# Transposing q and k by DMA as 16-bit halves, from the fifth pair of heads on

## The chip, the cores and the metric

The kernel runs on one core of a Trainium2 chip. The metric is the device time of one execution in microseconds (us), lower is better. Before the change the median of three runs is 1266.16 us (1265.27 to 1266.54).

## The reference

Attention that keeps only the 32 largest scores of each row, followed by a small network on the result. There are 8 batches, 8 heads, 576 positions and 64 values per head.

```python
scores = 1/sqrt(64) * q @ k.T                  # (8, 8, 576, 576)
kth    = 32nd largest score of each row
attn   = softmax(scores where scores >= kth)
x      = (attn @ v), heads side by side        # (4608, 512)
h      = max(x @ w1, x @ w2, x @ w3)           # (4608, 768)
out    = h @ w_out                             # (4608, 512)
```

## The kernel before

**Tiling.** Heads are worked on in pairs: with 64 values per head, two heads fill the 128 partitions. Each pair has four units of 128 query rows; the 64 rows left over of two pairs make a fifth unit. That is 144 units in all. For a unit, TensorE computes the scores of both heads into PSUM (`qk`, L531), ScalarE copies them to SBUF (`evac`, L539), VectorE and GpSimd find the 32nd largest value (the lines up to L614), VectorE masks (L637), ScalarE takes the exponential (L646), TensorE transposes the result with an identity matrix (`turn`, L692), ScalarE copies the transposes out (L704), and TensorE multiplies with v (`values`, L723). Three small steps after it (L733 on VectorE, L747 on ScalarE, L751 on GpSimd) put the attention result into x as two 16-bit parts. When all heads of a batch have done a span of rows, the network runs on the span: L780 is its first layer, L840 the second, L845 and L851 write the result.

**What the change touches: preparing q and k.** The scores need q and k with the 64 values of a head along the partitions. Today `load_qk` brings both from memory as they lie (L445; L449 for the last 64 rows), and `prep` returns three steps. Step one transposes the last rows on TensorE (L474) and copies them out (L477). The two others, for k and then for q, are four transposes each on TensorE (L483), a scaled copy from PSUM into the one buffer `raws` (L487), a rounding copy into `kT` or `qT` (L488), and a subtraction on GpSimd that leaves the rounding error (L492). The score product uses both parts. `kT` and `qT` have two buffers; `raws`, `qt`, `kt` and `last` have one. A pair is prepared once, but those of the first batch twice, so there are 36 preparations, which `prepare(pi)` numbers in order.

**What sets the order.** The program is not written in order of time. Every step is a `Piece` with an engine, an estimated cost, the steps that it needs, the ring buffers that it takes and a rank (the unit that it belongs to, plus a number of `OFFSETS` by kind of step). `in_order` plays the pieces on a model of the five engines, and the order in which the model starts them is the order of each engine's instructions. Every engine, and SP, which issues all transfers, then works in that order, whatever the real times are. The model takes a result of another engine to be seen after the step's cost, that engine's `LATE` (2000 ns for SP) and `GAP`. The pieces of the network are a list of their own (`fill`): on TensorE they are looked at last, so they take the time that attention leaves.

**End.** The units of the last batch are ordered so that its first 256 rows are complete first, then the next 256, then the last 64. The network on these three spans ends the program.

Of the kernel before, what the change touches and what calls it, by code (L numbers as in the profile page):

```python
# [8 lines left out]
F32 = mybir.dt.float32  # L9
F32R = mybir.dt.float32r  # L10
F16 = mybir.dt.float16
BF16 = mybir.dt.bfloat16
I32 = mybir.dt.int32
AF = mybir.ActivationFunctionType
ALU = mybir.AluOpType
AX = mybir.AxisListType
# [8 lines left out]
NSSB = 5  # L25
NWB = 6
PMB = 2
GAP = 104.0
NEAR = 162.0
SWITCH = 95.0  # L30
WINDOW = 150
LEAD = 42.7
LOCK_A = -150.0
LOCK_B = -100.0
OFFSETS = {'E0': -5.5, 'E1': 2.05, 'E2': 2.82, 'N': -0.93, 'T0': 0.58, 'T1': 5.15, 'T2': 2.73, 'Y': -1.06, 'Z': -0.03, 'd': -3.25,
# [8 lines left out]
RANK_M = -20.0  # L44
LATE = {'PE': 160.0, 'DVE': 85.0, 'ACT': 100.0, 'POOL': 40.0, 'SP': 2000.0}

# [21 lines left out]
def in_order(pieces, fill):  # L68

    queues, fills = {e: [] for e in LATE}, {e: [] for e in LATE}
    for x in sorted(pieces, key=lambda x: x.rank):
        queues[x.engine].append(x)
    for x in fill:
        fills[x.engine].append(x)
    free = {e: 0.0 for e in LATE}
    mode, shut = [None], [0.0]

    def ready(x):  # L80
        t = free[x.engine]
        for y in x.needs:
            if y.start is None:
                return None
            t = max(t, y.seen(x.engine))
        ahead = {}
        for ring, releases in x.takes:
            k = len(ring.users) - ring.size + ahead.get(ring, 0)
            ahead[ring] = ahead.get(ring, 0) + 1
            for y in ring.users[k] if k >= 0 else ():  # L90
                if y.start is None:
                    return None
                t = max(t, y.seen(x.engine))
        if x.engine == "PE" and x.mode != mode[0]:
            t += SWITCH

        if x.alone:
            t = max(t, free["POOL"] + LOCK_A)
        elif x.engine == "POOL":
            t = max(t, shut[0] + LOCK_B)  # L100
        return t

    left = len(pieces) + len(fill)
    while left:
        best = None
        low = min((q[0].rank for q in queues.values() if q), default=0.0)
        for e in LATE:
            some = [x for x in queues[e][:WINDOW] if x.rank <= low + LEAD]
            some = some + fills[e][:1] if e == "PE" else fills[e][:1] + some
            could = [(t, x) for x in some if (t := ready(x)) is not None]  # L110
            if could:
                first = min(t for t, _ in could) + PATIENCE[e]
                t, x = next(c for c in could if c[0] <= first)
                if best is None or t < best[0]:
                    best = t, x
        assert best, [(e, len(q), len(fills[e])) for e, q in queues.items()]
        t, x = best
        (fills if fills[x.engine][:1] == [x] else queues)[x.engine].remove(x)
        x.start = t
        free[x.engine] = t + x.cost  # L120
        if x.engine == "PE":
            mode[0] = x.mode
        if x.alone:
            shut[0] = t + x.cost
        for ring, releases in x.takes:
            ring.users.append(releases)
        x.run()
        left -= 1


PATIENCE = {'PE': 97, 'DVE': 158, 'ACT': 0, 'POOL': 0, 'SP': 0}


@with_exitstack
def kernel(ctx, tc, q, k, v, moe_w1, moe_w2, moe_w3, moe_w_out, out):
# [8 lines left out]
    KC = DM // P  # L144
    FC = DF // P
    HALF = S // 2
    HALF_SCALE = (SHRINK / float(D) ** 0.5) ** 0.5
    MAIN = NU * P
    WIDE = S - 2 * P
    HW = WIDE + 64  # L150
# [311 lines left out]
    def prep(b, hp):  # L462
# [11 lines left out]
            nc.tensor.transpose(pt[:, 0:P], both[2].rearrange("p h d -> p (h d)"), ident)  # L474

        def rest_out():
            nc.scalar.activation(raws[:, S:].rearrange("p (w n) -> p w n", n=64)[:, ::C], box["rest"][:, 0:P].rearrange("p (w n) -> p w n", w=2), AF.Copy,  # L477
                                 scale=HALF_SCALE)

        def products(w):  # L480
            pt = box[w] = ps_t.tile([P, 512], F32, name="tr")
            for c in range(NU):
                nc.tensor.transpose(pt[:, c * P:(c + 1) * P], both[w][:, c].rearrange("p h d -> p (h d)"), ident)  # L483

        def split(w):
            raw, t = (raw_of_q, raw_of_k)[w], (qT[:, 0, 0:S + 64], kT[:, 0])[w]
            nc.scalar.activation(raw[:, 0:MAIN], box[w], AF.Copy, scale=HALF_SCALE)  # L487
            nc.scalar.copy(t, raw)  # L488

        def rest_of(w):  # L490
            raw, t, low = (raw_of_q, raw_of_k)[w], (qT[:, 0, 0:S + 64], kT[:, 0])[w], (qT[:, 1, 0:S + 64], kT[:, 1])[w]
            nc.gpsimd.tensor_tensor(low, raw, t.bitcast(F32), ALU.subtract)  # L492
        return [(rest, rest_out, None)] + [(lambda w=w: products(w), lambda w=w: split(w), lambda w=w: rest_of(w)) for w in (1, 0)]

    which = [1]
    spots = const.tile([P, NW], F32, name="spots")
# [37 lines left out]
    def evac(n):  # L534
        d = st[n]
        s = d["s"]
        t = wk.tile([P, 2, S], F32, name="ssb", bufs=NSSB)
        d["ssb"] = [t[:, 0], t[:, 1]]
        nc.scalar.copy(t.rearrange("p h (i n) -> p h i n", i=2), s[:, :, :, :HALF])  # L539

    def sweep(n, i):

# [363 lines left out]
    def attention(n):  # L906
# [17 lines left out]
            opened[b] = []  # L924
            takes.append(("books", opened[b]))
        p("q", "PE", 786 if full else 1572, lambda: qk(n), needs=[x for k in preps_of[n] for x in prepared[k]], takes=takes, mode="rows")
        p("e", "ACT", 1060, lambda: evac(n), needs=[d["q"]], takes=[("ssb", held(n, "ssb"))])
        rel.append(d["e"])
        for i in range(2):
            p(("s", i), "DVE", 1184 - 296 * i, lambda i=i: sweep(n, i), needs=[d["e"]] + ([d["s", 0]] if i else []),  # L930
# [86 lines left out]
    def prepare(pi):  # L1017
        b, hp = preps[pi]
        rank = starts[pi]
        load = piece("SP", 4000, lambda: load_qk(b, hp), list(load_last), rank, tag="ql" if pi else "ql0")  # L1020
        box = {}
        load_last.clear()
# [2 lines left out]
        for k in range(3):  # L1025
# [3 lines left out]
                box["turns"][k][0]()  # L1029
            rel = []  # L1030
            x = piece("PE", 140 if k == 0 else 436, products, [load, *done[-1:]], rank, [("tr", rel)], tag="qp")
            y = piece("ACT", 220 if k == 0 else 1206, lambda k=k: box["turns"][k][1](), [x, *last, *done[-1:]], rank, tag="qp")
            rel.append(y)
            load_last.append(x)
            if pi >= 2:
# [5 lines left out]
                load_bits.append(z)  # L1041
        prepared[pi] = done

    load_bits = []

    def finish(b):
# [120 lines left out]
```

## Time and profile before

| | |
|---|---|
| median of 3 runs | 1266.16 us |
| the profiled execution | 1265.52 us |
| its span, first to last instruction | 1263.8 us |
| TensorE (PE) busy | 1190.5 us, 94% |
| VectorE (DVE) busy | 1139.0 us, 90% |
| ScalarE (ACT) busy | 1057.1 us, 84% |
| GpSimd (POOL) busy | 927.2 us, 73% |
| mean granted TensorE clock | 0.988 of 2.4 GHz |

The busy times are sums over the span, which has three parts that differ: about 100 us of start, in which the weights are brought in and converted, a long even stretch, and an end in which TensorE works alone. PEld is TensorE's loading of weights, which runs beside its products. Durations of TensorE's instructions overlap, so what one of them costs is the distance from its start to the start of the next, not its length.

### The profile page before, as it was taken

What the parts mean: (1) busy time and instruction counts of PE and PEld (TensorE: products, weight loads), DVE (VectorE), ACT (ScalarE), POOL (GpSimd) and SP (SyncE); (2) the same over time, 40 slices, a digit from 0 to 9 for tenths busy, and PEclk for the clock granted to TensorE, in tenths of its full rate; (3) what the DMA queues carried; (4) which work ended last, traced back from release to release, by engine and by line L of the source; (5) the groups of instructions that cost most, each with busy time, mean ns of one, the idle gap of its engine ahead of it and who ended that gap; (6) DMA issues with size and microseconds to landing.
All of it is one profiled execution on the core that took longest, in us unless ns stands there. A gap on an engine that the chain in (4) does not pass through costs nothing.

```text
span 1263.8 us, 32126 instructions
## 1 busy us (share of the span) xinstructions
PE 1190.5 (94%) x10431; PEld 882.2 (70%) x10431; DVE 1139.0 (90%) x5558; ACT 1057.1 (84%) x2382; POOL 927.2 (73%) x1443
## 2 busy tenths in 40 slices
PE   4677789999999999999999999999999999999997
PEld 2455567878686766767687777867776767767775
DVE  7899999999999999999999999999999999999221
ACT  2799899999998988899899999898998889888321
POOL 1667778788888786878878788877787888868111
PEclk9999899999999999999999999999999999999999
DMA  8440111111111110011111111100110111000000
GB/s 274 140 139 20 38 38 49 39 38 38 38 30 46 30 38 27 21 50 26 46 30 46 30 39 46 30 28 20 53 42 28 30 29 37 2 18 2 18 18 29
DMA packets 112401, 54.86 MB, mean 43 GB/s; under 512 B 96608, under 2 KB 104800, under 8 KB 112224
## 3 DMA queue, kind: packets, MB, share of 16 engines
q1 hardware_dynamic: 112224, 52.72, 15.2%
q8 instruction: 84, 1.38, 0.4%
q14 instruction: 93, 0.76, 0.2%
HBM read 43.25 MB, written 9.44 MB: 42 GB/s over the span
## 4 chain that ended last, share of the span: by engine, by line
PE 71%; DVE 17%; ACT 8%; issue 2%; POOL 1%; DMA 1%; SPq 0%; ACTq 0%; DVEq 0%; POOLq 0%
PE m L780 28%; PE tr L723 11%; PE s L531 10%; PE m L840 10%; PE tr L692 8%; DVE L L548 4%; DVE ssb L637 4%; DVE Q L596 2%; PE tr L483 2%; ACT pm L646 2%; ACT w L587 2%; PE tr L687 1%; ACT pT L704 1%; DVE h L789 1%; ACT ssb L539 1%
## 5 line engine op out<-in xcount | busy, mean ns | idle before, releaser
L592 POOL TENSOR_TENSOR w<-ssb,w 128x576 f32<-128x576 f32 x288 | 425.9, 1485 | 51.4 <-ACT w L587 47.7
L780 PE MATMUL m<-xh,wall 128*128 128x256 f16 (+4 forms) x2592 | 441.7, 273 | 2.2 <-DVE h L789 1.3
L780 PEld LDWEIGHTS <-wall 128*128 128x128 f16 x3888 | 354.5, 98 | 76.4 <-issue 11.7
L780 PE MATMUL m<-xl,wall 128*128 128x256 f16 (+4 forms) x1296 | 345.1, 273 | 0.0
L548 DVE MAX8 L<-ssb 128x8 f32<-128x82 f32 (+1 forms) x2016 | 317.2, 227 | 3.1 <-ACT ssb L539 3.1
L637 DVE SCALAR_TENSOR_TENSOR ssb<-ssb,kth 128x576 f32<-128x576 f32 x288 | 262.3, 923 | 0.2
L646 ACT ACTIVATE pm<-ssb,nb 128x576 f32<-128x576 f32 x288 | 224.5, 781 | 29.8 <-DVE ssb L637 29.3
L704 ACT COPY pT<-tr 128x512 f32<-128x512 f32 (+1 forms) x432 | 215.0, 515 | 31.6 <-PE tr L692 17.9
L587 ACT ACTIVATE w<-ssb,Q 128x576 f32<-128x576 f32 x288 | 223.0, 777 | 14.2 <-DVE Q L580 12.2
L596 DVE MAX8 Q<-w 128x8 f32<-128x576 f32 x288 | 214.1, 748 | 5.0 <-POOL w L592 4.7
L692 PE MATMUL tr<-ident,pm 128*128 128x128 f32 x1152 | 179.3, 282 | 11.4 <-ACT pm L646 6.6
L531 PE MATMUL s<-kT,qT 64*128 64x288 f32 x1920 | 173.1, 316 | 14.4 <-ACT ssb L539 8.5
L723 PE MATMUL tr<-pT,vt 128*64 128x256 f32 (+2 forms) x2000 | 179.3, 328 | 2.7 <-ACT s L192 1.9
L531 PEld LDWEIGHTS s<-kT,qT 64*128 64x128 f32 x1920 | 137.7, 192 | 58.8 <-ACT ssb L539 19.5
L539 ACT COPY ssb<-s 128x1152 f32<-128x1152 f32 x144 | 161.5, 1121 | 14.5 <-PE s L531 13.7
L789 DVE SCALAR_TENSOR_TENSOR h<-m,rises,h 128x256 f32<-128x256 f32 (+4 forms) x216 | 102.8, 476 | 74.5 <-PE m L780 68.5
L692 PEld LDWEIGHTS tr<-ident,pm 128*128 128x128 f32 x1152 | 131.3, 142 | 51.4 <-issue 14.6
L723 PEld LDWEIGHTS tr<-pT,vt 128*64 128x64 f32 x2000 | 112.0, 139 | 60.8 <-issue 13.3
L795 POOL TENSOR_TENSOR hl<-h,hh 128x256 f16<-128x256 f32 (+4 forms) x108 | 83.8, 776 | 83.8 <-ACT hh L792 82.8
L840 PE MATMUL m<-wall,hh 128*128 128x512 f16 x432 | 128.6, 379 | 0.0
L661 POOL TENSOR_SCALAR rsw<-rs 128x128 f32<-128x128 f32 x144 | 62.1, 431 | 27.9 <-DVE rs L656 10.8
L840 PE MATMUL m<-wall,hl 128*128 128x512 f16 x216 | 81.9, 379 | 0.0
(124 smaller groups left out, 1648.9 us busy)
## 6 DMA issues: line engine op xcount, KB each, us to landing
qt<-in_q_dram SPq DMA_DIRECT2D x72, 128.0 KB, 2.8
kt<-in_k_dram SPq DMA_DIRECT2D x72, 128.0 KB, 3.0
out_dram<-ob SPq DMA_DIRECT2D x32, 256.0 KB, 2.3
wall<-in_moe_w_dram SPq DMA_DIRECT2D x8, 768.0 KB, 6.2
vt<-in_v_dram SPq DMA_DIRECT2D x32, 128.0 KB, 2.1
vt<-in_v_dram SPq DMA_DIRECT2D x32, 64.0 KB, 2.2
vt<-in_v_dram SPq DMA_DIRECT2D x96, 16.0 KB, 2.0
vt<-in_v_dram SPq DMA_DIRECT2D x32, 48.0 KB, 2.1
```

The costliest lines, as they stand in the source:

```text
L531: nc.tensor.matmul(s[:, h, i, :HALF], qT[sl, qa, c0:c0 + P], kT[sl, ka, i * HALF:(i + 1) * HALF], start=(n_ == 0 and a == 0), stop=(n_ == ...
L548: nc.vector.max(d["L"][:, t, g, :], d["ssb"][t][:, g * S // G:(g + 1) * S // G])
L587: nc.scalar.activation(d["w"][t], d["ssb"][t], AF.Sign, bias=d["Q"][:, t, 0:1], scale=-1.0, accum_out=d["cnt"][:, t:t + 1])
L592: nc.gpsimd.tensor_tensor(d["w"][t], d["ssb"][t], d["w"][t], ALU.mult)
L596: nc.vector.max(d["Q"][:, t, 1:NW], d["w"][t])
L637: nc.vector.scalar_tensor_tensor(ss, ss, d["kth"][:, t:t + 1], ss, ALU.is_lt, ALU.subtract, accum_out=d["lost"][:, t:t + 1])
L646: nc.scalar.activation(d["pm"][:, t], d["ssb"][t], AF.Exp, bias=d["nb"][:, t:t + 1], scale=-1.0 / SHRINK, accum_out=d["sums"][:, t:t + 1])
L692: nc.tensor.transpose(pt[:, j * P:(j + 1) * P], pm[:, i, 64 * i + j * P:64 * i + (j + 1) * P], ident)
L704: nc.scalar.copy(pT[:, 512 * i:512 * i + m] if i < 2 else pT[:, 8 * P:10 * P], pt[:, :m])
L723: nc.tensor.matmul(xp[64 * h:64 * h + 64, to], vt[:, 4 * h + i if i < 4 else 8 + h, :], keys, start=(i == 0), stop=(i == 4))
L780: nc.tensor.matmul(box["ps", i][:, :c1 - c0], a, bb[:, kc, c0:c1], start=(kc == 0 and k == 0), stop=(kc == KC - 1 and k == 2))
L840: nc.tensor.matmul(box["po"][:n], a[:, f, cs], bb, start=(f == 0 and k == 0), stop=(f == FC - 1 and k == 2))
```

## The change

From preparation 4 on (`BY_DMA = 4`, so 32 of 36), TensorE no longer transposes q and k. Instead, for k and then for q:

- `load`: SP issues two transposing transfers, one per head. The 576x64 32-bit numbers are read as 576x128 16-bit numbers and arrive as 128x576, with the low halves of the numbers in the even partitions and the high halves in the odd ones.
- `gather`: SP issues four transfers from SBUF to SBUF, which collect the low halves and the high halves of both heads in one tile `halves` of 128 partitions x 2 x 576.
- `split`: ScalarE joins the halves in `raws` by two copies of 16-bit numbers, of 1024 and of 128 per partition.
- `high`, `low`: the rounding copy on ScalarE and the subtraction on GpSimd, as before.

The two transposed tiles and `halves` have one buffer each. The factor that was put on q and on k (its square root on each) goes on the scores, in the copy from PSUM. The order's constants and all `OFFSETS` are set anew, and TensorE in a mode (the score products, the products with v) prefers to stay in it for up to `STICK` ns of the model.

```diff
-GAP = 104.0
-NEAR = 162.0
-SWITCH = 95.0
+GAP = 106.0
+NEAR = 167.0
+SWITCH = 100.0
+STICK = 191.0
-LEAD = 42.7
+LEAD = 62.6
...
-                first = min(t for t, _ in could) + PATIENCE[e]
-                t, x = next(c for c in could if c[0] <= first)
+                first = min(t for t, _ in could)
+                stays = [c for c in could if c[1].mode and c[0] <= first + STICK] if e == "PE" and mode[0] else []
+                t, x = stays[0] if stays else next(c for c in could if c[0] <= first + PATIENCE[e])
...
-PATIENCE = {'PE': 97, 'DVE': 158, 'ACT': 0, 'POOL': 0, 'SP': 0}
+PATIENCE = {'PE': 103, 'DVE': 161, 'ACT': 16, 'POOL': 21, 'SP': 0}
...
-            nc.scalar.activation(raw[:, 0:MAIN], box[w], AF.Copy, scale=HALF_SCALE)
+            nc.scalar.copy(raw[:, 0:MAIN], box[w])
...
+        def load(w):
+            tiles = box["tiles"] = [io.tile([P, S], U16, name=nm, bufs=1) for nm in ("qt", "kt")]
+            for h in range(2):
+                nc.sync.dma_start(tiles[h], (q, k)[w][b, 2 * hp + h].bitcast(U16), transpose=True)
+
+        def gather(w):
+            both = box["both"] = io.tile([P, 2, S], U16, name="halves", bufs=1)
+            for h in range(2):
+                for t in range(2):
+                    nc.sync.dma_start(both[64 * h:64 * h + 64, t, :], box["tiles"][h][t::2, :])
+
+        def split(w):
...
+            words = raw.bitcast(U16)
+            nc.scalar.copy(words[:, 0:2 * MAIN].rearrange("p (c n t) -> p c n t", c=NU, t=2),
+                           both[:, :, 0:MAIN].rearrange("p t (n c) -> p c n t", c=NU))
+            end = raw.shape[1]
+            nc.scalar.copy(words[:, 2 * (end - 64):2 * end].rearrange("p (n t) -> p n t", t=2), both[:, :, MAIN:S].rearrange("p t n -> p n t"))
...
-        nc.scalar.copy(t.rearrange("p h (i n) -> p h i n", i=2), s[:, :, :, :HALF])
+        nc.scalar.activation(t.rearrange("p h (i n) -> p h i n", i=2), s[:, :, :, :HALF], AF.Copy, scale=SCALE)
...
-        p("e", "ACT", 1060, lambda: evac(n), needs=[d["q"]], takes=[("ssb", held(n, "ssb"))])
+        p("e", "ACT", 1170, lambda: evac(n), needs=[d["q"]], takes=[("ssb", held(n, "ssb"))])
...
+        if pi >= BY_DMA:
+            steps = turned_prep(b, hp)
+            done, last, before = [], list(load_bits), list(load_last)
+            load_bits.clear()
+            for w in (1, 0):
+                load, gather, split, high, low = ((lambda f=f, w=w: f(w)) for f in steps)
+                x = piece("SP", 4300, load, before, rank, tag="ql")
+                y = piece("SP", 3000, gather, [x, *free_halves], rank, tag="qm")
+                before = [y]
+                z = piece("ACT", 1150, split, [y, *last, *done[-1:]], rank, tag="qs")
+                users[pi - 2].append(z)
+                free_halves[:] = [z]
+                h = piece("ACT", 610, high, [z], rank, tag="qp")
+                lo = piece("POOL", 1420, low, [h], rank, tag="qp")
+                done += [h, lo]
+                load_bits.append(lo)
+            load_last[:] = before
+            prepared[pi] = done
+            return
```

## Rows read from the trace of the kernel before

**Rows 1.** By stretch: busy PE, PEld, DVE, ACT, POOL (instructions); clock, DMA share, GB/s.
```profile
100.00:1150.00 1050.00, 1019.61 (x9046) 760.28 (x9046) 1014.92 (x5078) 950.65 (x2148) 849.47 (x1316) 0.99 0.13 34
...
1181.00:1259.00 78.00, 75.18 (x739) 58.33 (x737) 16.33 (x43) 17.10 (x42) 10.33 (x19) 1.00 0.06 20
```

**Rows 2.** The chain that ended last, from 1181 us: start, us, what.
```profile
1183.79 20.96 PE m L780 x192
1204.75 7.77 PE m L840 x36
1212.52 23.58 PE m L780 x216
1236.10 7.79 PE m L840 x36
```

**Rows 3.** By stretch, L780 alone: busy PE, PEld (instructions); clock, DMA share, GB/s.
```profile
1153.00:1181.00 28.00, 10.03 (x67) 6.24 (x66) 1.00 0.03 11
```

**Rows 4.** The same with L840 alone.
```profile
1153.00:1181.00 28.00, 8.59 (x36) 3.51 (x36) 1.00 0.03 11
```

**Rows 5.** Timeline: the last step of the last batch's first 256 rows.
```profile
1152.81 1.17 POOL L751 TENSOR_TENSOR xl<-xs,xh 128x256 f16<-128x256 f32 x1 [0.71 <-ACT xh L747]
```

**Rows 6.** Timeline of PE: the transposes of q and k, each with its successor.
```profile
597.09 0.60 PE L483 MATMUL tr<-ident,kt 128*128 128x128 f32 x4
...
597.53 0.43 PE L780 MATMUL m<-xh,wall 128*128 128x320 f16 x2
...
626.71 0.27 PE L474 MATMUL tr<-ident,last 128*128 128x128 f32 x1
...
626.82 0.59 PE L840 MATMUL m<-wall,hh 128*128 128x512 f16 x2
```

**Rows 7.** The transposes of q: ns min/median/max, first and last start, shape.
```profile
L483 PE MATMUL tr<-ident,qt x144: 271/273/421, 18.5 to 1088.6; 128*128 128x128 f32 x144
```

**Rows 8.** Groups of ACT, shapes apart: busy us, mean ns, idle before and releaser.
```profile
L704 ACT COPY pT<-tr 128x512 f32<-128x512 f32 x288 | 166.2, 584 | 25.9 <-PE tr L692 17.9 <-DVE xs L733 4.6 <-DVE kth L614 1.4
L539 ACT COPY ssb<-s 128x1152 f32<-128x1152 f32 x144 | 161.5, 1121 | 14.5 <-PE s L531 13.7
L487 ACT ACTIVATE raws<-tr 128x512 f32<-128x512 f32 x72 | 43.1, 599 | 11.5 <-PE tr L483 11.0
L845 ACT ACTIVATE ob<-m,so 128x512 f32<-128x512 f32 x32 | 22.1, 692 | 14.2 <-PE m L840 14.1
L477 ACT ACTIVATE raws<-tr 128x128 f32<-128x128 f32 x36 | 10.4, 288 | 16.7 <-PE tr L474 16.7
```

**Rows 9.** Who waited for whom on DVE and ACT, 100 to 1150 us: us, times, longest.
```profile
DVE h L789 <- PE m L780: 15.1, 37, 1.3
DVE xs L733 <- PE tr L723: 5.1, 9, 1.6
ACT pm L646 <- DVE ssb L637: 28.4, 34, 2.7
ACT w L587 <- DVE Q L580: 11.5, 14, 3.1
ACT raws L487 <- PE tr L483: 6.9, 12, 1.1
```

**Rows 10.** DMA issues: KB each, median us from issue to landing.
```profile
qt<-in_q_dram SPq DMA_DIRECT2D x72, 128.0 KB, 2.8
vt<-in_v_dram SPq DMA_DIRECT2D x32, 64.0 KB, 2.2
```

**Rows 11.** Timeline of SP: one load of q and k.
```profile
612.75 1.25 SPq L445 DMA_DIRECT2D qt<-in_q_dram  x2
```

**Rows 12.** DMA queue: packets, MB, share of 16 engines.
```profile
q1 hardware_dynamic: 112224, 52.72, 15.2%
```

**Rows 13.** One line of each batch's review: first and last start, for the batch period.
```profile
L669 DVE TENSOR_TENSOR junk<-Q,kth x8: 476/492/1599, 207.6 to 1171.0; 128x324 f32<-128x324 f32 x8
```

**Rows 14.** Who waited for whom on SP's queue: us in total, times, longest.
```profile
SPq L851 <- ACT ob L845: 206.4, 23, 37.2
```

More of the change, by code (lines that the diff above doesn't have):

```diff
@@ L13 @@
 I32 = mybir.dt.int32
+U16 = mybir.dt.uint16
 AF = mybir.ActivationFunctionType
@@ L27 @@
 PMB = 2
-GAP = 104.0
-NEAR = 162.0
-SWITCH = 95.0
+GAP = 106.0
+NEAR = 167.0
+SWITCH = 100.0
+STICK = 191.0
 WINDOW = 150
-LEAD = 42.7
+LEAD = 62.6
 LOCK_A = -150.0
 LOCK_B = -100.0
-OFFSETS = {'E0': -5.5, 'E1': 2.05, 'E2': 2.82, 'N': -0.93, 'T0': 0.58, 'T1': 5.15, 'T2': 2.73, 'Y': -1.06, 'Z': -0.03, 'd': -3.25,
[8 rows of a table removed]
+OFFSETS = {'E0': -6.34, 'E1': -0.03, 'E2': 1.48, 'N': -1.36, 'T0': -2.57, 'T1': 6.25, 'T2': 2.95, 'Y': 1.38, 'Z': -0.59, 'd':
[9 rows of a table added]
 RANK_M = -20.0
@@ L146 @@
     HALF = S // 2
-    HALF_SCALE = (SHRINK / float(D) ** 0.5) ** 0.5
+    SCALE = SHRINK / float(D) ** 0.5
     MAIN = NU * P
@@ L476, in rest_out @@
         def rest_out():
-            nc.scalar.activation(raws[:, S:].rearrange("p (w n) -> p w n", n=64)[:, ::C], box["rest"][:, 0:P].rearrange("p (w n) -> p w n", w=2), AF.Copy,
-                                 scale=HALF_SCALE)
+            nc.scalar.copy(raws[:, S:].rearrange("p (w n) -> p w n", n=64)[:, ::C], box["rest"][:, 0:P].rearrange("p (w n) -> p w n", w=2))
         def products(w):
@@ L493, in prep, with turned_prep, high, low @@
         return [(rest, rest_out, None)] + [(lambda w=w: products(w), lambda w=w: split(w), lambda w=w: rest_of(w)) for w in (1, 0)]
+    def turned_prep(b, hp):
+        box = {}
+        def load(w):
[8 more added lines that the diff above has]
+        def split(w):
+            if w:
+                which[0] ^= 1
+                T_of[b, hp] = qTs[which[0]], wk.tile([P, 2, S], F32R, name="kT")
+            both = box["both"]
+            raw = (raw_of_q, raw_of_k)[w]
+            words = raw.bitcast(U16)
[3 more added lines that the diff above has]
+            nc.scalar.copy(words[:, 2 * (end - 64):2 * end].rearrange("p (n t) -> p n t", t=2), both[:, :, MAIN:S].rearrange("p t n -> p n t"))
+        def high(w):
+            qT, kT = T_of[b, hp]
+            nc.scalar.copy((qT[:, 0, 0:S + 64], kT[:, 0])[w], (raw_of_q, raw_of_k)[w])
+        def low(w):
+            qT, kT = T_of[b, hp]
+            to, t = (qT[:, 1, 0:S + 64], kT[:, 1])[w], (qT[:, 0, 0:S + 64], kT[:, 0])[w]
+            nc.gpsimd.tensor_tensor(to, (raw_of_q, raw_of_k)[w], t.bitcast(F32), ALU.subtract)
+        return load, gather, split, high, low
     which = [1]
@@ L1031, in prepare @@
             x = piece("PE", 140 if k == 0 else 436, products, [load, *done[-1:]], rank, [("tr", rel)], tag="qp")
-            y = piece("ACT", 220 if k == 0 else 1206, lambda k=k: box["turns"][k][1](), [x, *last, *done[-1:]], rank, tag="qp")
+            y = piece("ACT", 160 if k == 0 else 1080, lambda k=k: box["turns"][k][1](), [x, *last, *done[-1:]], rank, tag="qp")
             rel.append(y)
@@ L1042, in prepare @@
         prepared[pi] = done
+    BY_DMA = 4
+    free_halves = []
     load_bits = []
```

17 rows, old and new, of the table OFFSETS are left out of this document.

## Prediction

> **What bounds the kernel now.** I read the busy time by stretch first, because the page's shares are averages over a start, an even stretch and an end. From 100 to 1150 us PE is busy 1019.6 of 1050 us, DVE 1014.9, ACT 950.7 and POOL 849.5 [rows 1]: two engines at 97%, ACT at 91%. From 1181 us on DVE and ACT are nearly idle and PE has 75.2 of 78 us [rows 1]. The chain of waits says what that end is: first layer and second layer of the network on 256 rows (20.96 and 7.77 us), on the next 256 rows (23.58 and 7.79), and a short one on the last 64 [rows 2]. So when attention ends, at 1181 us, the whole network of the last batch is still to do.
>
> It is still to do because the network takes only what attention leaves of PE, and PE has been behind: between 1153 and 1181 us it spends 10.0 us in L780 and 8.6 us in L840 [rows 3, 4], and those belong to the batch before. The last batch's first 256 rows are complete only with the subtraction that starts at 1152.81 us [rows 5]. The end is thus set by two things, the moment at which attention ends (DVE, with ACT close behind) and the work that PE has left by then.
>
> **What PE loses.** In the timeline four transposes of k start at 597.09 us and the next instruction at 597.53, so four cost 0.44 us though each is listed with more; the one of the last rows costs 0.11 us (626.71 to 626.82) [rows 6]. A preparation has two fours and one single: 0.99 us. 32 of 36 preparations lose them: 31.7 us of PE, all before 1089 us, where the last of them starts [rows 7]. The stickiness in a mode may save some more; no row prices it, and by what follows PE could not use it.
>
> **What of it is worth time.** With attention's own times kept, the freed PE time goes to the network, which then reaches the last batch earlier. But the last batch's first rows cannot be used before 1153 us. To be free for them then, PE must have done the 18.6 us of older network work (10.0 + 8.6) that now lies between 1153 and 1181. Of the 31.7 us freed, 18.6 do this; the other 13.1 become idle time before 1153. In its place 18.6 us of the last batch's first layer move in front of 1181 us, and the end comes 18.6 us earlier. I take 1 us off for the beginning of that layer, which now has to run between attention steps: 17.6 us gained. Lower end: nothing, if the order does not move the work forward. Upper end: all 31.7, if attention's last units come earlier too.
>
> **What ACT gets.** Removed per preparation: a 128-wide copy at 288 ns and two 512-wide at 599 [rows 8], 1486 ns. Added, twice: a copy of 1024 numbers and one of 128. No row shows 16-bit numbers read with strides. By width the rows give 584 ns for 512 and 1121 for 1152 [rows 8], 0.839 ns per number, so 1014 for 1024; the small one is 288. Twice 1302 is 2604, and 2604 - 1486 = 1118 ns, times 32: 35.8 us. Bounds for the wide copy are half and double of 1014, since 16-bit numbers may go faster and strides may cost: 3 to 101 us for the sum. I take the middle, as the copy at L477 also writes with a stride and costs no more than its width. The scale in the copy of the scores: the scaled copy of 512 at L487 takes 599 ns, the plain one of the same shape 584 [rows 8], 15 ns, times 144: 2.2 us. The upper bound is the scaled copy at L845, 692 ns, whose factor is read from a tile: 108 ns, 15.6 us. I take 2.2, the same kind of factor. The sum is 38 us of ACT, 91% to about 94% in the even stretch.
>
> What reaches the end of attention? At most all 38 us. Below nothing: DVE waits 15.1 us for L780 and 5.1 us for L723 on PE [rows 9], and a freer PE can take those 20 us away. I take +4 us, a tenth of ACT's: ACT has 99 us idle there (1050 - 950.7) [rows 1], 28.4 and 11.5 us of it in waits for DVE [rows 9], where ACT's being later costs nothing, and its waits of 6.9 us for the removed transposes [rows 9] go. POOL's subtraction stays as it was; DVE gets nothing.
>
> **What the transfers cost.** They are hidden as long as they land before ACT's order wants them. Per operand: two transposing loads, then four gathers that wait for them on SP. No row shows either kind. Nearest rows: a plain load of 128 KB lands after 2.8 us, one of 64 KB after 2.2 [rows 10]; SP issues one in about 0.62 us [rows 11]. That makes 0.6 + 2.8 = 3.4 us and 3 x 0.6 + 2.2 = 4.0 us, 7.4 us per operand. The diff's model books 4300 ns for the loads and 3000 + 2000 + 106 until ACT may use the gathers: 9.4 us, 2.0 more. The other end: if a transfer moved each 16-bit number as a packet of its own, at 27 ns per packet (15.2% of 16 x 1263.8 us over 112224 packets [rows 12]), 73,728 of them on 16 engines would take 126 us. I take the low end, the row of equal size. The batch period is (1171.0 - 207.6) / 7 = 137.6 us [rows 13], 34.4 us per pair, against 2 x 7.4 for its two operands through the single buffers. A split that waits holds up everything behind it in ACT's queue: the copies of the scores, the signs and the exponentials, and so DVE. Output stores and loads of v stand behind a waiting gather on SP; SP waits 206.4 us in 23 waits for results to store [rows 14], so a few us there push nothing.
>
> The low end agrees with the Trainium skill's "Advanced Engine Details and Errata", X-Bar Transpose, which has these transfers as fast as plain ones; no run here shows one yet. Against the change stands its "VectorE: DVE Perf Modes", The three transpose paths: a 128x128 block of 16-bit numbers takes 390 ns on TensorE and 1309 ns by DMA; by that (an estimate) a load of 576x128 takes 5.9 us and two in turn 11.8.
>
> **Sum.** Profiled execution 1265.5 - 17.6 + 4 = 1251.9 us. The median of the runs is 0.6 above that execution, so 1252.
>
> **The rivals.**
> *Attention gets faster as well.* DVE's 20 us of waits for PE speak for it, ACT's 38 us against it. With about 14 of those 20 gone and nothing from ACT: 1265.5 - 17.6 - 14 + 0.6, about 1234.
> *ACT becomes the bound (slower).* Place: ACT's queue in the even stretch. For it: 94% beside a DVE at 97%, in fixed order, so waits need not move where they are cheap. Against it: the 99 us idle. It turns slower when more than 17.6 of the 38 us, 46%, reach the end of attention; with three quarters (28.5 us) 1265.5 - 17.6 + 28.5 + 0.6 = 1277.
> *The transposing loads land late (slower).* Place: the wait of `split`, 64 times. Each us over the booked 9.4 us per operand costs ACT 64 us; idle time of 99 us and the gain of 17.6 are used up at (99 + 17.6) / 64 = 1.8, that is from 11.2 us per operand on. With two loads one after another at twice the row's landing time (11.2 us) and 4.0 for the gathers it is 5.8 us over: 371 us of waits, less 99 and 17.6, some 1520 us. By the skill page's 1309 ns the case would be this one. The rows, with 2.0 us to spare, speak against it.
> *The freed time finds no use.* If the network's pieces fall into the same places, PE is only idler before 1181 us: 1266. For it: attention's steps come first in the order, and the last rows are late anyway. Against it: the network's list is always waiting.
>
> **How the numbers follow.** Forecast 0.52 (its own range 1243 to 1261), attention faster too 0.15, no use 0.10, ACT as the bound 0.15, late transposes 0.08. Within 0.2% (1263.6 to 1268.7), about what a measurement of this kernel can tell from no change, lies only the fourth rival: faster 0.67, same 0.10, slower 0.23. The range leaves out the late transposes and the outer parts of the first two rivals: 1230 to 1282.
>
> **What would show it.** In the profile after: PE's busy time some 30 us less; gaps on PE before about 1150 us, none of size in the end; first-layer products of the last batch before attention ends; from DVE's last attention step to the end about 60 instead of 78 us. ACT busy about 1095 us, its wide 16-bit copies near 1014 ns, the copy of the scores near 1136. The loads landing near 3 us, and hardly any wait of the joining copies for a transfer. I am wrong if those copies wait for DMA by 1 us or more each, if they take 2 us, or if attention ends later than about 1195 us.

## The result: slightly slower, not faster

The change takes 1272.05 us (median of 5 runs, 1271.16 to 1276.04) against 1265.27 us before in the same comparison: ratio 1.0063, 95% interval 1.0041 to 1.0084. Forecast were 1252 us. The profiled execution took 1271.62 us, 1269.8 us of them span.

The page of the kernel after, totals and shares of the chain:

```profile
span 1269.8 us, 31937 instructions
...
PE 1169.3 (92%) x10143; PEld 851.2 (67%) x10143; DVE 1158.5 (91%) x5558; ACT 1110.1 (87%) x2414; POOL 921.2 (73%) x1443
...
PE 60%; DVE 23%; ACT 11%; issue 2%; POOL 2%; DMA 1%; ACTq 0%; DVEq 0%; POOLq 0%
```

TensorE has lost 21.2 us of work and is a smaller part of the chain (60%, before 71%). ScalarE has 53.0 us more, and VectorE, whose instructions the change does not touch, 19.5 us more. The same stretches as in [rows 1], after:

```profile
100.00:1150.00 1050.00, 996.50 (x8709) 728.22 (x8707) 1017.07 (x5009) 991.50 (x2153) 831.04 (x1297) 0.98 0.20 52
1181.00:1259.00 78.00, 77.40 (x804) 61.45 (x802) 22.57 (x62) 23.01 (x57) 15.06 (x29) 1.00 0.05 18
```

In the even stretch TensorE was freed (53.5 us idle, before 30.4), yet in it the kernel got less far. The best ruler for that is the step that VectorE does once per batch ("review", [rows 13]), after:

```profile
L709 DVE TENSOR_TENSOR junk<-Q,kth x8: 466/818/1728, 212.0 to 1186.6; 128x324 f32<-128x324 f32 x8
```

The last two figures are the first and the last start. The span is first review, plus seven batch periods, plus the tail after the last review. Before: 207.6 + 7 x 137.6 + 92.8. After: 212.0 + 7 x 139.2 + 83.2. So the beginning lost 4.4 us and the seven batches 11.2, attention being 15.6 later; the tail gained 9.6; sum +6.0, which is the difference of the spans. The tail, by the chain, against [rows 2]:

```profile
1196.55 14.41 PE m L820 x132
1210.96 7.77 PE m L880 x36
1218.73 23.58 PE m L820 x216
1242.32 7.78 PE m L880 x36
```

Of the first layer on the last batch's first 256 rows, 6.6 us less are left here (14.41 instead of 20.96), and this rest starts 10.0 us after the last review instead of 12.8; together that is nearly all of the 9.6 us. So a part has moved in front of attention's end, about half of what was forecast. Attention's last subtraction (L791) now starts at 1195.25 us, before at 1181.83 (L751): beyond the 1195 from which I had called the prediction wrong.

The part has moved because attention's end went back, not because the network came forward. The first product of the network for the last batch, in the timelines of TensorE before and after:

```profile
1180.89 0.39 PE L780 MATMUL m<-xh,wall 128*128 128x256 f16 x2
```

```profile
1180.74 0.38 PE L820 MATMUL m<-xh,wall 128*128 128x256 f16 x2
```

The network reached the last batch at the same moment as before. What TensorE was freed of became idle time: 53.5 instead of 30.4 us in the even stretch.

What the new steps cost, by groups of ScalarE and by transfers (KB, median us to landing):

```profile
L579 ACT ACTIVATE ssb<-s 128x1152 f32<-128x1152 f32 x144 | 164.1, 1140 | 11.3 <-PE s L571 10.6
L520 ACT COPY raws<-halves 128x1024 uint16<-128x1024 uint16 x64 | 98.0, 1531 | 0.0
L523 ACT COPY raws<-halves 128x128 uint16<-128x128 uint16 x64 | 20.9, 326 | 0.0
...
halves<-qt SPq DMA_DIRECT2D x128, 72.0 KB, 2.1
halves<-kt SPq DMA_DIRECT2D x128, 72.0 KB, 2.2
...
qt<-in_k_dram SPq DMA_TRANSPOSE x32, 2.6
```

The joins never wait (idle before them: 0.0), so the transfers are hidden. A wide join takes 1531 ns, not 1014. Who waits for whom, 100 to 1150 us, after:

```profile
PE tr L732 <- ACT pm L686: 17.5, 14, 3.5
...
ACT w L627 <- DVE Q L620: 15.2, 18, 2.0
ACT pm L686 <- DVE ssb L677: 12.0, 14, 1.8
...
DVE h L829 <- PE m L820: 11.3, 26, 1.7
```

and the first of these lines before:

```profile
PE tr L692 <- ACT pm L646: 4.8, 8, 1.0
```

Before, TensorE waited 4.8 us for those exponentials, now 17.5; ScalarE waited 28.4 us for the masks [rows 9], now 12.0: ScalarE, which used to be early towards VectorE, is now late towards TensorE.

### The profile page after: what moved, and what is told of

It is laid out like the page before. It is cut to its first block, busy times and chain, and to the rows that moved or that the text cites. A ratio compares the mean times of both kernels' runs of the same rounds, so it can differ in the third digit from the quotient of the medians.

```text
span 1269.8 us, 31937 instructions
## 1 busy us (share of the span) xinstructions
PE 1169.3 (92%) x10143; PEld 851.2 (67%) x10143; DVE 1158.5 (91%) x5558; ACT 1110.1 (87%) x2414; POOL 921.2 (73%) x1443
## 4 chain that ended last, share of the span: by engine, by line
PE 60%; DVE 23%; ACT 11%; issue 2%; POOL 2%; DMA 1%; ACTq 0%; DVEq 0%; POOLq 0%
PE m L820 26%; PE tr L763 9%; PE s L571 8%; PE tr L732 8%; PE m L880 7%; DVE L L588 6%; DVE ssb L677 5%; DVE Q L636 3%; ACT pm L686 2%; ACT w L627 2%; ACT pT L744 2%; DVE h L829 2%; ACT raws L520 1%; PE tr L727 1%; ACT ssb L579 1%
## 5 line engine op out<-in xcount | busy, mean ns | idle before, releaser
L820 PEld LDWEIGHTS <-wall 128*128 128x128 f16 x3888 | 355.9, 98 | 79.4 <-issue 12.2
L677 DVE SCALAR_TENSOR_TENSOR ssb<-ssb,kth 128x576 f32<-128x576 f32 x288 | 273.2, 957 | 0.1
L686 ACT ACTIVATE pm<-ssb,nb 128x576 f32<-128x576 f32 x288 | 226.5, 787 | 13.6 <-DVE ssb L677 12.9
L744 ACT COPY pT<-tr 128x512 f32<-128x512 f32 (+1 forms) x432 | 218.1, 517 | 17.5 <-PE tr L732 7.7
L763 PE MATMUL tr<-pT,vt 128*64 128x256 f32 (+2 forms) x2000 | 184.3, 334 | 3.6 <-ACT pT L744 3.4
L579 ACT ACTIVATE ssb<-s 128x1152 f32<-128x1152 f32 x144 | 164.1, 1140 | 11.3 <-PE s L571 10.6
L520 ACT COPY raws<-halves 128x1024 uint16<-128x1024 uint16 x64 | 98.0, 1531 | 0.0
```

The costliest lines, as they stand in the source:

```text
L677: nc.vector.scalar_tensor_tensor(ss, ss, d["kth"][:, t:t + 1], ss, ALU.is_lt, ALU.subtract, accum_out=d["lost"][:, t:t + 1])
L686: nc.scalar.activation(d["pm"][:, t], d["ssb"][t], AF.Exp, bias=d["nb"][:, t:t + 1], scale=-1.0 / SHRINK, accum_out=d["sums"][:, t:t + 1])
L744: nc.scalar.copy(pT[:, 512 * i:512 * i + m] if i < 2 else pT[:, 8 * P:10 * P], pt[:, :m])
L763: nc.tensor.matmul(xp[64 * h:64 * h + 64, to], vt[:, 4 * h + i if i < 4 else 8 + h, :], keys, start=(i == 0), stop=(i == 4))
L820: nc.tensor.matmul(box["ps", i][:, :c1 - c0], a, bb[:, kc, c0:c1], start=(kc == 0 and k == 0), stop=(kc == KC - 1 and k == 2))
```

## Experiments

"Attention's end" below is the start of the last review; times are medians, and intervals belong to the ratio to the kernel before in the same comparison.

**1. The join by itself.** A program with nothing but forms of the copy, twelve of each (it computes none of the reference's outputs). The forms, in short:

```diff
+ copy(a "p (c n t)", both "p t (n c) -> p c n t")   # as_is: the change's form
+ copy(b "p (n t)",   both "p t n -> p n t")         # plain_in: numbers left in their order
+ copy(c, both as it lies)                           # flat_both
+ copy(d, halves as the outer loop)                  # t_outer; two_steps: one copy per half
+ copy(f, the same bytes as 512 words of 32 bits)    # words; then as_is on GpSimd and VectorE
```

> Leaves out the whole computation: twelve copies in a row of 1024 16-bit numbers on ACT in each of several orders, and the same on POOL and DVE; the profile is read, not the time. Theory A (the halves as the innermost dimension cost, because each number read lies 1152 bytes from the one before): about 1530 ns in the form of the change, about 1040 ns (0.839 ns per number) for 1024 numbers read in a row and for the order with the halves outermost. Theory B (16-bit numbers are slow on ACT in any order): about 1530 ns in every 16-bit form, 590 ns for 512 32-bit numbers. Theory C (it is contention inside the kernel): about 1040 ns in all 16-bit forms here.

```profile
L63 DVE COPY dve_as_is<-halves 128x1024 uint16<-128x1024 uint16 x12 | 22.0, 1835 | 0.4
L57 POOL COPY pool_as_is<-halves 128x1024 uint16<-128x1024 uint16 x12 | 21.6, 1801 | 1.6 <-DVE halves L26 1.6
...
L42 ACT COPY as_is<-halves 128x1024 uint16<-128x1024 uint16 x12 | 18.0, 1497 | 0.0
L51 ACT COPY two_steps<-halves 128x512 uint16<-128x512 uint16 x24 | 16.5, 753 | 0.0
L48 ACT COPY t_outer<-halves 128x1024 uint16<-128x1024 uint16 x12 | 16.0, 1333 | 0.0
L44 ACT COPY plain_in<-halves 128x1024 uint16<-128x1024 uint16 x12 | 13.8, 1152 | 0.0
L46 ACT COPY flat_both<-halves 128x1024 uint16<-128x1024 uint16 x12 | 12.5, 1039 | 0.0
L54 ACT COPY words<-halves 128x512 f32<-128x512 f32 x12 | 7.3, 604 | 0.0
```

The 1531 ns belong to the form itself: it takes 1497 without the kernel around it. Width alone is 1039 (the estimate was 1014). Taking the halves alternately adds 113, and picking every fourth number, which puts the four units' rows together, the other 345. So theory A's times for the change's form and for numbers in a row came, but its reason covers only the 113: the form with the halves outermost takes 1333, not 1040.

**2. Shorter joins in the changed order.** First the copy without that reordering (rows of a pair land in other places, so the output is another); then 512 words of older q and k in place of the wide join (scores of wrong rows). Neither moves an instruction. In short:

```diff
-  copy(words "p (c n t)", both "p t (n c) -> p c n t")
+  copy(words "p (n t)",   both "p t n -> p n t")          # e5
+  copy(raw[:, 0:MAIN], box["old"][w][:, 0, 0:MAIN])       # e6
```

> The changed kernel, order of every engine kept; the joining copy reads and writes its numbers in natural order, so the main columns of q and k are permuted. By the forms measured alone it is 0.35 us shorter, 64 times: 22 us less of ACT. If ACT's joining copies set the end of attention: 1258 to 1267. If the order does, with ACT hidden: 1269 to 1274.

> The changed kernel, order kept; in place of the 1024 halves the copy takes 512 32-bit numbers of the q and k prepared before, so q and k are wrong. About 0.6 instead of 1.53 us, 64 times: 59 us less of ACT, which is also below what the kernel before spends there. If ACT's joining copies are the cause: attention ends before 1185 us and the time is 1242 to 1256. If the new order is the cause: above 1265.

e5: 1271.78 us, 1.0056 (1.0042 to 1.0069), ScalarE busy 1090.7. e6: 1276.26 us, 1.0093 (1.0079 to 1.0107), ScalarE 1062.1, no busier than before the change. Both lie in the range of "the order does it". Taking away 48 us of ScalarE's work gave nothing. In the changed order ScalarE's length does not set the time; my first theory, that the dear join did, falls.

**3. More ScalarE, or less TensorE, in the order of before.** e7 does the scaled copy of q and k twice. e8 leaves out the sets of four transposes of q and k from the fifth preparation on (the single ones of the last rows stay) and copies older data instead (wrong scores). e15 does e8 and that copy three times, which comes near the change's loads (22 us more on ScalarE) in the order of before.

```diff
+            for _ in range(2):                                                        # e7
             nc.scalar.activation(raw[:, 0:MAIN], box[w], AF.Copy, scale=HALF_SCALE)
+            if old: return                     # e8, e15: no sets of four transposes
+            src = old[0][:, 0, 0:MAIN] if old else box[w]
+            for _ in range(3 if old else 1):   # e15 alone
```

> The kernel before, order kept; the copy at L487 is done twice, which adds about 0.5 us of ACT 72 times, 36 us (what I had forecast for the change). If ACT is nearly a bound there: 1274 to 1290. If its 99 us of idle time take it up, as my +4 us said: 1265 to 1270.

> The kernel before, order kept; from the fifth preparation on the 64 sets of four transposes are left out and the copy takes earlier q values from SBUF, so q and k are wrong. 28 us less of PE with nothing added to ACT. If PE is the bound wherever it is busy: 1237 to 1248. If a fixed order lets PE only wait a little earlier and the network stays where it stood: 1256 to 1264.

> The kernel before, order kept, with both loads of the change and none of its transfers: the 64 sets of transposes left out as in the run without them, and the copy that follows done three times, about 64 us more of ACT; q and k are wrong. If the two loads add up as they were measured alone (less 12 us for TensorE, 20/36 us per us of ACT): 1280 to 1292. If ACT's load is hidden: 1252 to 1262.

e7: 1284.53 us, 1.0161 (1.0147 to 1.0175), in the range of "nearly a bound"; its second copy also keeps the PSUM buffer longer, which e15's copies from SBUF do not. e8: 1252.71 us, 0.9903 (0.9888 to 0.9919), between its two ranges. e15: 1313.72 us, 1.0379 (1.036 to 1.0398), some 22 above the highest expectation. Their totals and reviews, first e8:

```profile
PE 1165.2 (93%) x10175; PEld 853.2 (68%) x10175; DVE 1137.9 (91%) x5558; ACT 1055.2 (84%) x2382; POOL 928.0 (74%) x1443
...
L675 DVE TENSOR_TENSOR junk<-Q,kth x8: 480/528/1586, 209.4 to 1160.5; 128x324 f32<-128x324 f32 x8
```

and e15:

```profile
PE 1184.2 (90%) x10175; PEld 861.5 (66%) x10175; DVE 1149.6 (88%) x5558; ACT 1132.5 (86%) x2510; POOL 924.1 (70%) x1443
...
L676 DVE TENSOR_TENSOR junk<-Q,kth x8: 474/492/1152, 223.8 to 1219.4; 128x324 f32<-128x324 f32 x8
```

e8 has the time that I forecast for the change, but not for the reason: its tail is 1253.0 - 1160.5 = 92.5 us, as before. The freed TensorE made attention itself faster (10.5 us by the last review). And e15 has nowhere near a full ScalarE (86%), but 77.3 us more of its work cost 61.0 us of time: the 99 us of idle time that I counted as cover cover next to nothing as long as the order stays.

**4. VectorE's and TensorE's share.** In the order of before: a fill of two numbers after each mask (e9), one more maximum in a quarter of the units (e16). In the changed order: one maximum less per unit (e10), three of seven first maxima over 41 numbers instead of 82 (e13), the third product of the split scores left out for half of the keys (e17). e10 and e13 find wrong thresholds, e17 has less exact scores (for the second half of the keys, not the first, as its expectation says), and in all three a constant stops the second pass that the kernel makes when it is in doubt. e14, the same as e17 without that constant, made that pass, so its 4180.43 us compare with nothing; its first pass had the last review at 1171.3.

```diff
+        nc.vector.memset(idle[:, 0:2], 0.0)                              # e9
...
+        for _ in range(2 if t == 0 and n % 4 == 0 else 1):               # e16
             nc.vector.max(d["Q"][:, t, 1:NW], d["w"][t])
...
-            for t in range(2): nc.vector.max(b9s[n % 3][:, t, 1:9], ...)
+            nc.vector.max(b9s[n % 3][:, 0, 1:9], ...)                    # e10
...
+                end = g * S // G + 41 if i else (g + 1) * S // G         # e13
...
-  for n_, (qa, ka) in enumerate(((0, 0), (0, 1), (1, 0))):
+  for n_, (qa, ka) in enumerate(((0, 0), (0, 1), (1, 0))[:3 - i]):       # e17
...
+    nc.vector.memset(flag_i, 0)                                          # e10, e13, e17
```

> The kernel before, order kept; after each of the 288 masks VectorE does one more tiny instruction, a fill of two numbers per partition (60 ns, 17 us in all: about what VectorE has more in the changed kernel). Theory DVE (VectorE is the bound of attention, and the change's loss is VectorE's longer work): 1276 to 1284. Rival (some us more on VectorE are taken up by its idle time): 1264 to 1270.

> The kernel before, order kept; in every fourth unit one maximum over 576 columns is done twice, which follows at 0.67 us: 24 us more of VectorE that nothing overlaps. If VectorE is a bound of attention: 1278 to 1290. If it is hidden: 1264 to 1268.

> The changed kernel, order kept; one of the two maxima of the first pivot step is left out (172 ns, 144 times: 25 us less of VectorE), and the second pass over the input is switched off, so the thresholds of every second head are wrong. Theory DVE: 1245 to 1256. Rival (in the changed kernel TensorE's waits or ScalarE set attention's end): 1265 to 1274.

> The changed kernel, order kept; six of the fourteen maxima of each unit's sweep read 41 columns instead of 82, and the second pass is switched off, so thresholds are wrong. About 43 ns off 864 instructions that follow each other: 37 us less of VectorE in real distance. If VectorE sets the end of attention in the changed kernel: 1240 to 1255. If it does not: 1265 to 1273.

> The changed kernel, its order unchanged, with the third product of the split scores left out for the first half of the keys (some 26 us of PE; those scores are less exact), as in the run before it of this kind, and with the second pass over the input switched off by a constant, so that the time is that of one pass. In the first pass of that earlier run the last review started at 1171.3 us against 1186.6 with the change. Theory 'PE still sets the pace of the changed order': the last review again near 1171 and the time 12 to 20 us under the change, 1252 to 1260. Rival 'no engine alone holds it, DVE most': under 5 us gained, 1267 to 1272; the earlier first pass would then have been shortened by something else.

| | busy time changed by | time | ratio (95%) | us per us |
|---|---|---|---|---|
| e9, before's order | VectorE +2.2 | 1264.70 | 0.9997 (0.9988 to 1.0006) | dose too small |
| e16, before's order | VectorE +31.2 | 1287.32 | 1.0180 (1.0164 to 1.0195) | 0.7 |
| e7, before's order | ScalarE +37.4 | 1284.53 | 1.0161 | 0.5 |
| e15 against e8 | ScalarE +77.3 | 1313.72 | 1.0379 | 0.8 |
| e8, before's order | TensorE -25.3 | 1252.71 | 0.9903 | 0.5 |
| e17, changed order | TensorE -19.9 | 1262.26 | 0.9978 (0.9966 to 0.9991) | 0.5 |
| e13, changed order | VectorE -26.6 | 1263.86 | 1.0001 (0.9992 to 1.0010) | 0.3 |
| e10, changed order | VectorE -8.8 | 1269.27 | 1.0035 (1.0022 to 1.0048) | 0.3 |
| e6, changed order | ScalarE -48.0 | 1276.26 | 1.0093 | nothing |

(Change of the median over change of the page's busy time; for the changed order against 1272.05. Busy time counts overlapped work once and holds what other instructions gained or lost: e9's 288 fills are 17.3 us by themselves, the 144 maxima that e10 leaves out 24.6.) e16 lies in the range of "a bound", e9 and e10 in their rivals', e13 and e17 between their ranges. The review of e17, to be held against that of the change:

```profile
L709 DVE TENSOR_TENSOR junk<-Q,kth x8: 476/819/1725, 211.8 to 1176.1; 128x324 f32<-128x324 f32 x8
```

None of ScalarE, VectorE and TensorE sets the time alone. Work added to ScalarE or VectorE in the order of before cost 0.5 to 0.8 us per us (e9 apart); work taken away gave 0.5 back on TensorE, 0.3 on VectorE and nothing on ScalarE, the last two in the changed order only. GpSimd was not tried.

**5. The order alone.** The change also sets the planner's constants anew. e2 has them with the old way of transposing, e3 has the new way with the constants of before; e4 books the join in the planner at what it takes. e11, e12 and e18 move one constant by the least that counts, `GAP`, by 1 ns.

```diff
-    BY_DMA = 4
+    BY_DMA = 36                                   # e2
-GAP = 106.0 ... OFFSETS = {...}
+GAP = 104.0 ... OFFSETS = {... of before}         # e3, with no STICK
-                z = piece("ACT", 1150, split, ...
+                z = piece("ACT", 1640, split, ... # e4
+GAP = 105.0                                       # e11, on the kernel before (104)
+GAP = 107.0                                       # e12, on the change (106); 105.0 in e18
```

> The new constants and the scale on the scores, but all 36 preparations by TensorE as before. If the joining copies on ACT make the change slow: no joining copies, ACT busy about 1060 us, attention ends near 1181 us, time 1258 to 1267. If the new constants make it slow: the late start and the later end of attention stay, time 1270 to 1285, and PE has its 32 us back on top.

> The transfers and joining copies of the change with the old constants, offsets and no stickiness. If the joining copies make it slow: ACT busy about 1110 us, time 1268 to 1285, not faster than the changed kernel. If the new constants make it slow: start and batch period as before the change, the end about 18 us shorter, time 1247 to 1262.

> The changed kernel with the joining step booked at 1640 ns in the model (two starts 1.63 us apart in its trace) instead of 1150; nothing else. If it is the wrong booking that makes ACT run late of the plan 64 times: 1255 to 1265. If it is ACT's load itself, whatever the plan knows: 1268 to 1276.

> The kernel before with GAP 105 instead of 104 in the model, nothing else: the same work in another order. If the orders are interchangeable: 1262 to 1268. If the old order is a lucky one out of many: 1274 to 1290, like the other orders tried.

> The changed kernel with GAP 107 instead of 106 in the model, nothing else. If the orders are interchangeable: 1269 to 1275. If the new order is a lucky one: 1280 to 1292. If it is an unlucky one: below 1266.

> The changed kernel with one constant of the order's planner (the gap of 107 ns between instructions) set to 105; nothing else. A second neighbour of the changed order, for the spread among orders of the same work. Theory 'an order fitted to its durations is worth 10 to 20 us, any replan loses it': 1274 to 1288. Rival 'the change costs what its work costs, orders matter little': within 3 us of the change, 1269 to 1275.

| transposed by | order | time | ratio (95%) | last review | tail |
|---|---|---|---|---|---|
| TensorE | before | 1265.27 | 1 | 1171.0 | 92.8 |
| TensorE | GAP 105 (e11) | 1274.97 | 1.0087 (1.0074 to 1.0101) | 1180.7 | 93.4 |
| TensorE | new constants (e2) | 1284.22 | 1.0148 (1.0123 to 1.0173) | 1190.0 | 92.4 |
| DMA | the change | 1272.05 | 1.0063 (1.0041 to 1.0084) | 1186.6 | 83.2 |
| DMA | GAP 105 (e18) | 1271.26 | 1.0048 (1.0034 to 1.0062) | 1186.5 | 83.6 |
| DMA | GAP 107 (e12) | 1275.49 | 1.0094 (1.0076 to 1.0111) | 1188.0 | 85.9 |
| DMA | join booked 1640 (e4) | 1285.65 | 1.0155 (1.0131 to 1.0178) | 1192.5 | 87.5 |
| DMA | old constants (e3) | 1285.93 | 1.0159 (1.0136 to 1.0182) | 1204.1 | 83.8 |

Read across the constants first. Under those of before, the transposes by DMA are 20.7 us slower (e3); under the new ones, 12.2 us faster (the change against e2; the ratios of the two comparisons give 21 and 11). Each way of transposing is better under the constants set for it, so the kernel before and the change are both fitted orders, and what the forecast set against each other, the work, was compared here through two different fits. One nanosecond in one constant, the work being the same, moved the kernel before by 10 us, and the change by 1 to 4 (e18 starts from 106; the 107 in its expectation is a slip). e2, e11 and e18 lie in a range that was expected (new constants slow, old order a lucky one, orders of the change alike), e12 and e3 less than 1 us above one; e4 lies above both of its ranges, so the wrong booking was not what made the change slow.

The columns on the right show what is common to the orders. With DMA the tail is shorter in each, 83 to 88 us against 92 to 93. Relative to the last review the network is further on, its first product for the last batch starting 0.3 to 9.8 us before that review instead of 10 us after it. But in time it is hardly earlier: that product starts at 1176.7 to 1198.2 us with DMA, at 1180.9 to 1199.9 with TensorE. The last review is later on average (1191.5 against 1180.6), but the ranges overlap. On average the two ways take 1275 and 1278 us. These orders are few and some of them near relatives, so this says only that the difference between the two ways is smaller than the spread among orders of one.

## Why the prediction was wrong

**Which step failed.** "What reaches the end of attention? ... I take +4 us, a tenth of ACT's." Attention's end came 15.6 us later. This is 11.6 of the 19.6 us between -13.6 (forecast) and +6.0 (spans). The other 8.0 are the first term: of 17.6 us of tail, 9.6 came.

**The first term failed in its mechanism too.** "With attention's own times kept, the freed PE time goes to the network, which then reaches the last batch earlier." The times were not kept, and the network reached the last batch at 1180.7 us, before at 1180.9. Of the freed time I had taken 13.1 us to become idle; in the even stretch TensorE was idle 23.1 us more, 12.7 of them in longer waits for the exponentials, while its work fell by 21.2 us in all. The 9.6 us of tail are the other side of attention's being late: the network kept its place while attention moved back.

**The reason behind +4** was that ScalarE's idle time, and its waits for VectorE, take up its added work. They don't: with the order kept, 37 to 77 us more cost half to four fifths of themselves (e7, e15), at 86% busy. Every engine works its list in a fixed order, so one that is late makes others wait where they had no slack, and idle time in other places is no use. That is the reading that fits; no run tests it on one wait alone. The change's new order, made around the new steps, got much of that back: 1272 us, where e15 has 1314 with 22 us more on ScalarE. But the new order has a price of its own: with ScalarE cut to its old load it stays at 1276 (e6), where the order of before with nearly the same loads takes 1253 (e8). So the relief of TensorE is worth 11.9 us where the order can stay (e8 against the kernel before in its comparison), and the order that makes room for the joins cost more than that. Shortening the joins afterwards gives nothing back in it (e5, e6), so within this order the 15.6 us are not the length of the joins; why it is dearer stays open.

The loss is not spread evenly. The seven batch periods were 144.1, 137.6, 141.5, 133.9, 136.3, 139.9 and 130.1 us and are 144.2, 140.6, 138.7, 139.6, 147.1, 134.5 and 129.9. The middle five hold 8 or 9 wide joins each and differ by -5.4 to +10.8 us, so the number of joins alone does not explain the loss.

**Two rivals that the traces speak against.** The granted clock of TensorE is lower after (0.972 instead of 0.988; 0.99 instead of 1.00 from the first to the last review). But the first period, in which it is lowest (0.94 instead of 0.99), took as long as before. The transfers (DMA share 0.20 instead of 0.13 in the even stretch) might slow the engines down: VectorE's maxima, which nobody changed, took 227 and 748 ns before and after, and most of what the mask gained is there without transfers too (e2 in the sums below).

**Where it shows in the trace**, in part, is the mask, a line that nobody changed and 10.9 of VectorE's 19.5 us. Before and after:

```profile
L637 DVE SCALAR_TENSOR_TENSOR ssb<-ssb,kth 128x576 f32<-128x576 f32 x288 | 262.3, 923 | 0.2
```

```profile
L677 DVE SCALAR_TENSOR_TENSOR ssb<-ssb,kth 128x576 f32<-128x576 f32 x288 | 273.2, 957 | 0.1
```

The masks that no work of GpSimd overlaps (17 before, 19 after) take 0.81 us on average in both kernels, the others 0.93 before and 0.97 after. In the timeline of before (start, us):

```profile
603.86 2.79 POOL L592 TENSOR_TENSOR w<-ssb,w 128x576 f32<-128x576 f32 x2
605.46 1.80 DVE L637 SCALAR_TENSOR_TENSOR ssb<-ssb,kth 128x576 f32<-128x576 f32 x1
...
609.39 0.79 DVE L637 SCALAR_TENSOR_TENSOR ssb<-ssb,kth 128x576 f32<-128x576 f32 x1
```

1.80 us with GpSimd's wide subtraction beside it, 0.79 when that is over. Summed over the masks, what lies above 0.82 us is 32.0 us before, 42.0 after, 47.4 in e6, 29.2 in e8; but 39.3 in e2 and 35.3 in e18, so it is a part of what an order is worth and not its measure. That GpSimd is the cause is read from who ran beside whom; no run took it away.

**Join.** Mis-sized: 1531 and 326 ns instead of 1014 and 288. ScalarE's busy time rose by 53.0 us, not 38. Picking every fourth 16-bit number costs more than the width; the bounds (507 to 2028) held, the middle did not. Cutting it afterwards gives nothing (e5 takes 19.4 us away and gains 0.3); whether a cheaper join planned from the start would, no run shows.

**TensorE.** By the page it lost 21.2 us, 25.3 in e8, where the forecast was 31.7 (28.2 for e8, which keeps the single transposes); the removed instructions are gone, but the others were listed longer. That the relief would go to the network and the tail is not borne out: in the change the network reached the last batch no earlier, and in the order of before (e8) the relief went wholly to attention, at 0.5 us per us, the tail staying at 92.5. I had counted this as a rival at 0.15.

**Scale in the copy of the scores.** Right: 1121 to 1140 ns, forecast 1136.

**Transfers.** Right: transposing loads land after 2.6 us, gathers after 2.1 to 2.2, and no join waits. The Trainium skill's "Advanced Engine Details and Errata", X-Bar Transpose, has such transfers as fast as regular ones, and the trace agrees (2.6 beside 3.0 to 3.1 us for the plain loads of q and k that are left in this profile). The estimate of 5.9 us from the Trainium skill's "VectorE: DVE Perf Modes", The three transpose paths, is not borne out: 4.5 blocks landed in 2.6 us. SP's part is dearer, 1.16 us to issue one (median) where a plain load took 0.62.

**Rivals.** By time "ACT becomes the bound" (1277) came nearest, but not by its mechanism: shorter joins gained nothing. "The freed time finds no use" comes nearest by mechanism: the network stands where it stood and TensorE is idler; what it left out is that attention gets later as well. It does not hold in general, since the order of before did use the relief (e8). "Late transposes" falls by the idle time of 0.0 before the joins.

**What would have told it in advance:** DVE 97%, TensorE 97% and ScalarE 91% busy in a fixed order, with 0.2 us of idle time before all 288 masks together. I read the small waits as slack that is there to be used; they were what a fitted order had left.

**Open.** Whether an order made anew for a cheap join, one that keeps numbers in their order, would bring attention back to e8's 1160. Nor was it shown which property of an order, overlap with GpSimd or the place of ScalarE's steps, makes it 10 us better. The later start (first review 212.0 against 207.6) decides nothing: e18 has 207.7 there and 1186.5 in the end. None of the kernels that do the whole work beats the kernel before.

## What to carry to other kernels

With several engines above 90% in an order fixed beforehand, price added work at half its length or more (ScalarE and VectorE here), and relief at no more than half, until an experiment says otherwise; idle time is cover only where the order lets the work reach it. Measure the spread of the order first (one constant of the planner by the smallest step): if it is 10 us, a change worth 10 us can't be judged from one order against one fitted order. Where freed time is to bring something forward, look whether that thing starts earlier in absolute time: here the tail got shorter and the network started when it had started before. A cheap test is the old order with the new loads put in as stand-ins: it separates what the work costs from what the new order costs.

## What the runs showed of the hardware

- ScalarE's time per number depends on how 16-bit numbers lie: 1024 of them take 1039 ns as they lie, 1152 with two rows taken alternately, 1497 with a step of four numbers too; the same bytes as 512 words 604.
- VectorE and GpSimd were slower beside each other. VectorE's mask took 0.79 and 1.80 us in the rows above (an extreme; the means are 0.81 and 0.93). GpSimd's copies in experiment 1, with VectorE's last copy ending at 24.4 us (timelines of VectorE, then of GpSimd):

```profile
2.04 22.40 DVE L63 COPY dve_as_is<-halves 128x1024 uint16<-128x1024 uint16 x12
...
21.66 2.10 POOL L57 COPY pool_as_is<-halves 128x1024 uint16<-128x1024 uint16 x1
23.70 1.94 POOL L60 COPY pool_outer<-halves 128x1024 uint16<-128x1024 uint16 x1
25.56 1.49 POOL L57 COPY pool_as_is<-halves 128x1024 uint16<-128x1024 uint16 x1
27.00 1.33 POOL L60 COPY pool_outer<-halves 128x1024 uint16<-128x1024 uint16 x1
```

The same copy takes 2.10 us while VectorE copies and 1.49 when it has ended, so the groups' 1801 ns above are means over both.
